# Softmax factors moved from the probabilities to the attention output, with PE spreading them over partitions

## The chip, the cores and the metric

The kernel runs on one core of a Trainium2 chip. The metric is the device time of one execution in microseconds (us). The core has five instruction streams that run beside each other: PE (matrix multiply), DVE (vector), ACT (activation functions), POOL (general vector) and SP (which only issues DMAs here). Each takes its instructions in order; semaphores hold an instruction back until its inputs are there or its buffer is free.

## The reference

Three stages follow each other. With B, H, S, D = 4, 8, 576, 64:

```
scores = q k^T / 8, causal, plus min(-(cum_i - cum_j), 0) with cum = cumsum(max(s, 0))
attn   = exp(scores - max) / (sum + 1e-9)
out    = attn v                                  # [B, H, S, D]
x  = out as [2304, 512]
h  = x @ w_in          [2304, 2048]
x  = (h * cos(h)) @ w_out                        # called FF1 below
xn = x / rms(x) * rms_g
out = (silu(xn @ w_gate) * (xn @ w_val)) @ w_out2  # called FF2 below
```

All inputs are fp32.

## The kernel before

**Tiling.** Attention goes by 16 pairs of heads. A pair has two parts: part a holds the first 256 queries (two tiles of 128 for each of the two heads), part b the other 320 (tiles 2 and 3 of each head, and a tile "p" that stacks the last 64 queries of both heads on the 128 partitions). For each tile PE makes scores (line 430 the product, 435 the bias; 457 and 458 for "p"), DVE copies them out of PSUM and finds the row minimum of the negated scores (442, 461), ACT takes the exponential in place and sums the row (469). The method norm (473) turns the row sums into factors: POOL forms (sum + 1e-9) * 2 pi (477), DVE takes the reciprocal (479), and each tile of exponentials is multiplied in place by its factor, one number to a partition, on DVE (485), ACT (486) or POOL (484). Then PE transposes the scaled tiles (500), ACT or DVE copies the transposes out of PSUM into P, PE multiplies by v (532) so that the output X has the head's 64 channels on partitions (head 0 on 0 to 63, head 1 on 64 to 127) and the queries along the row, and one copy takes X out of PSUM into xu (line 535, recorded under the helper's lines 286 on ACT and 289 on DVE). A DMA stores xu to DRAM.

**FF1** goes by 9 blocks of 256 rows. Its products are lines 634 (x w_in) and 640 (g w_out), each of them three fp32r products (high and low halves). Block 0 needs part a of the first four pairs, so FF1 can begin while attention still runs; PE alternates between the two from then on. During attention the weights of FF1 are also brought from DRAM and split into high and low halves: lines 361 to 371, on ACT or POOL (361, 362), POOL (365), DVE (366, 368) and helpers 286, 289, 293, 297 and 299 (tiles raw, cv, wi, ws). **FF2** goes by 6 blocks of 384 rows, with the same two kinds of product.

**What sets the order.** All work is recorded as operations with a cost in ns for each engine that may do it, a due time and the buffers read and written. A planner (Plan.order) walks through time, gives each operation to the engine that would end it first, and lets each engine take the ready operation with the earliest due time. The result is one fixed instruction order for each engine. Due times of attention advance by P_ATT (ns) per pair, those of FF1 by P_FF1 per unit from T_FF1. Four PSUM banks (4 to 7) serve attention; they are handed out in turn as the program records the operations, so an operation waits until the use of its bank four places earlier is done.

Of the kernel before, what the change touches and what calls it, by code (L numbers as in the profile page):

```python
# [10 lines left out]
F32 = mybir.dt.float32  # L11
F32R = mybir.dt.float32r
I32 = mybir.dt.int32
AF = mybir.ActivationFunctionType
ALU = mybir.AluOpType
# [24 lines left out]
HALF_PI = 1.5707962  # L40
BIG = 1.0e9
SIZES = {"u": 3, "xr": 1, "xa": 3, "xb": 2, "raw": 3, "P32": 4}
P_ATT, P_FF1, P_FF2 = 9000.0, 8093.98, 5800.0
T_FF1 = 45000.0


# [143 lines left out]
def dve1(n):  # L190
    return 1.042 * n + 67


def dve2(n):
    return 0.52 * n + 68


def act_s(n):
    return 0.833 * n + 93
# [6 lines left out]
def pool1(n):  # L206
    return 0.833 * n + 161


def pool2(n):  # L210
    return 2.105 * n + 147
# [3 lines left out]
def attention_moe_moe(ctx, tc, q2, k2, vp, s, w_in, w_out, w_gate, w_val, w_out2, rms_g, out):  # L215
    nc = tc.nc
    pe, act, dve, pool, sp = nc.tensor, nc.scalar, nc.vector, nc.gpsimd, nc.sync
    plan = Plan()

    def spool(stack, name, **kw):  # L220
        return stack.enter_context(tc.tile_pool(name=name, bufs=1, reuse_waits="tile", **kw))
# [3 lines left out]
    psum = spool(ctx, "psum", space=PSUM)  # L225
# [6 lines left out]
    def ring(name, n, shape, dtype, where="main"):  # L232
        n = SIZES.get(name, n)
        def make(slot):
            if where not in pools:
                first, kw = ends[where]
                stacks[first].close()
                pools[where] = spool(ctx, where, **kw)
            return pools[where].tile(shape, dtype, name=f"{name}{slot}", tag=f"{name}{slot}")

        r = Ring(plan, make, n)
        if where in ("main", "x1", "att"):
            for i in range(n):
                r.tile(i)
        return r
# [6 lines left out]
    ident = main.tile([128, 128], F32, name="ident")  # L252
# [27 lines left out]
    def on(e, ns, fn):  # L280
        return [(e, ns, fn)]

    def copy(o, i, n, r, w, scale=1.0, psum=False, engines=("ACT", "DVE", "POOL"), **kw):
        alts = []
        if "ACT" in engines:
            alts.append(("ACT", (act_p if psum else act_s)(n), lambda: act.activation(o(), i(), AF.Copy, scale=scale)))  # L286
        if "DVE" in engines:
            if scale == 1.0:
                alts.append(("DVE", (dve1 if psum else dve2)(n), lambda: dve.tensor_copy(o(), i())))
            else:  # L290
                alts.append(("DVE", dve2(n), lambda: dve.tensor_scalar(out=o(), in0=i(), scalar1=scale, scalar2=None, op0=ALU.mult)))
        if "POOL" in engines and not psum:
            alts.append(("POOL", pool1(n), lambda: pool.tensor_scalar(out=o(), in0=i(), scalar1=scale, scalar2=0.0, op0=ALU.mult, op1=ALU.add)))  # L293
        return plan.op(alts, r, w, **kw)

    def two(o, a, b, n, r, w, op=ALU.subtract, psum=False, **kw):
        alts = on("DVE", dve1(n), lambda: dve.tensor_tensor(out=o(), in0=a(), in1=b(), op=op))  # L297
        if not psum:
            alts += on("POOL", pool2(n), lambda: pool.tensor_tensor(out=o(), in0=a(), in1=b(), op=op))
        return plan.op(alts, r, w, **kw)  # L300
# [42 lines left out]
    xu_r = ring("xu", 3, [128, 320], F32, "att")  # L343
    p32_r = ring("P32", 4, [128, 4, 320], F32, "att")
    mn_r = ring("mn", 2, [128, 10], F32, "att")
    rs_r = ring("rs", 2, [128, 5], F32, "att")
    rn_r = ring("rn", 2, [128, 5], F32, "att")

    DS = {0: (0, 128), 1: (128, 256), 2: (384, 384), 3: (768, 512), "p": (1280, S)}
    x_d = [[{c: dbuf(f"x_d{b}_{p}{c}", [128, n]) for c, n in (("a", 256), ("b", 320))} for p in range(NP)] for b in range(B)]  # L350
# [52 lines left out]
    class Part:  # L403
# [7 lines left out]
            return psb("att", (4, 5, 6, 7))  # L411

        def stats(self):
            self.mn, self.rs, self.rn, self.xu = mn_r.new(), rs_r.new(), rn_r.new(), xu_r.new()

        def score(self, ts):

# [55 lines left out]
        def norm(self, keys):  # L473

            rn, rs, a = self.rn, self.rs, self.col[keys[0]]
            b = a + len(keys)
            plan.op(on("POOL", 204, lambda: pool.tensor_scalar(
                out=rn()[:, a:b], in0=rs()[:, a:b], scalar1=1e-9, scalar2=float(2.0 * np.pi), op0=ALU.add, op1=ALU.mult)), [(rs, self.col[k]) for k in keys], [(rn, a)])
            plan.op(on("DVE", 204, lambda: dve.reciprocal(out=rn()[:, a:b], in_=rn()[:, a:b])), [], [(rn, a)])
            for k in keys:  # L480
                (E, part, o, w), i = self.E[k], self.col[k]
                at, by = (lambda E=E, o=o, w=w: E()[:, o:o + w]), (lambda i=i: rn()[:, i:i + 1])
                plan.op([
                    ("POOL", 2.44 * w + 290, lambda at=at, by=by: pool.tensor_scalar(out=at(), in0=at(), scalar1=by(), scalar2=None, op0=ALU.mult)),
                    ("DVE", 0.62 * w + 110, lambda at=at, by=by: dve.tensor_scalar(out=at(), in0=at(), scalar1=by(), scalar2=None, op0=ALU.mult)),  # L485
                    ("ACT", act_s(w) + 93, lambda at=at, by=by: act.activation(at(), at(), AF.Copy, scale=by())),
                ], [(rn, a)], [(E, part)])

        def tr(self, e, i):
            tr = self.bank("T")  # L490
# [25 lines left out]

        def av(self):

            X, vr, P, n = self.bank("X"), self.run.vr, self.P, self.n

            def go():
                if self.c == "a":
                    ps = [P[e]().rearrange("p c i -> p (c i)") for e in range(2)]
                    jobs = [(0, 128, 0, 256, [p[:, 0:256] for p in ps]), (1, 128, 128, 256, [p[:, 256:384] for p in ps])]
                else:
                    ps = [P[e]() for e in range(2)]
                    jobs = [(c, 128, 0, 320, [p[:, c, :] for p in ps]) for c in range(3)]
                    jobs.append((3, 128, 128, 320, [p[:, 3, 128:320] for p in ps]))
                    jobs.append((4, 128, 256, 320, [p[:, 3, 0:64] for p in ps]))
                for c, kk, lo, hi, p in jobs:  # L530
                    for e in range(2):
                        pe.matmul(X()[64 * e:64 * e + 64, lo:hi], vr()[:kk, e, c, :], p[e], start=(c == 0), stop=(c == jobs[-1][0]))  # L532

            plan.op(on("PE", (640 if self.c == "a" else 2130) + SWITCH_PE, go), [vr, *P.values()], [X])
            copy(lambda: self.xu()[:, :n], lambda: X()[:, :n], n, [X], [self.xu], psum=True)

        def store(self):
            xu, n, xd = self.xu, self.n, x_d[self.run.b][self.run.p][self.c]
# [43 lines left out]
    for b in (s_b, cum):  # L582
# [4 lines left out]
        out=cum()[:, :S], data0=ones.to_broadcast([128, S]), data1=s_b()[:, :S], initial=0.0, op0=ALU.mult, op1=ALU.add)), [(s_b, 0)], [(cum, 0)])  # L587
# [6 lines left out]
    for i, (t, mid) in enumerate(((0, 63), (1, 191), (2, 319), ("p", 543), (3, 447))):  # L594
        o, w = DS[t]
# [9 lines left out]
            out=to(), in0=src(), scalar=halves[:, 1:2], in1=to().bitcast(F32), op0=ALU.mult, op1=ALU.add)), [raw], [(ds, o)], **kw)  # L605
# [75 lines left out]
    for j in range(1, NB1):  # L681
        for f in range(F1):
# [4 lines left out]
            w = w2[j, f] = ws_r.new() if j < RES else wr_r.new(f)  # L687
# [44 lines left out]
    for k in range(8 * NB1):  # L732
        j, m = divmod(k, 8)
# [5 lines left out]
        for i in range(2):  # L739
            plan.now = tick_at(k)  # L740
            w = w1[2 * m + i]
# [8 lines left out]
        for i in range(2):  # L750
            plan.now = tick_at(k) + 1.6 * P_FF1
            f = 2 * m + i
            w = w2[j, f]
# [46 lines left out]
    for n, (d, f, w) in enumerate((d, f, w) for f in range(F2) for d, w in (("g", w_gate), ("v", w_val), ("o", w_out2))):  # L800
# [4 lines left out]
        b = ws_r.new() if n < 4 else slots[n - 4][1].new(slots[n - 4][2])  # L805
# [4 lines left out]
    for n in range(NB2 * F2):  # L810
# [20 lines left out]
        w = w3["o", f]  # L831
# [4 lines left out]
        if f == F2 - 1:  # L836
            plan.now = unit_at(n)
            for t in range(3):
                o = u_r.new()
# [59 lines left out]
```

## Time and profile before

| what | value |
|---|---|
| median of 3 runs | 1107.75 us (1107.7 to 1108.04) |
| the profiled execution's own time | 1110.82 us |
| its span, first to last instruction | 1109.0 us |
| busy: PE, DVE, ACT, POOL | 97%, 49%, 48%, 17% |
| mean granted TensorE clock | 0.992 of full speed |

The span is what the profile shows; the execution's own time has 1.8 us around it. Busy shares are averages over unlike stages: attention, first alone and then with FF1 between its steps (to about 297 us), FF1 alone, and FF2. Matmuls overlap in PE, and their ends are modelled, so that PE shows as busy in stretches where it waits in part; the chain of waits (the instructions that ended last, followed backwards) tells better who set the pace of a stretch.

### The profile page before, as it was taken

The numbers are of one execution on the slowest core, as the hardware profiler recorded it, in microseconds if no ns is written. First come the engines' busy times: TensorE is split into PE (matmuls) and PEld (weight loads), VectorE is DVE, ScalarE is ACT, GpSimd is POOL, SyncE is SP. The second block draws the span as 40 slices with busy tenths as digits, with TensorE's granted clock in tenths as the row PEclk, the third lists the DMA queues.
The fourth block names the chain that finished last, engine by engine and source line by source line (L and its number), as shares of the span: only waits on it lengthen the run. The fifth ranks groups of instructions, "written<-read, shape, count | busy, mean of one in ns | idle before, by whom it ended". The sixth has DMA issues, their size and how long they took to land.

```text
span 1109.0 us, 16861 instructions
## 1 busy us (share of the span) xinstructions
PE 1080.4 (97%) x6474; PEld 938.8 (85%) x6474; DVE 547.1 (49%) x1209; ACT 528.7 (48%) x1098; POOL 187.1 (17%) x256
## 2 busy tenths in 40 slices
PE   8899999999999999999999999999999999999998
PEld 5568667777799999999998788999999999999997
DVE  6887998864474543535438888421211211211211
ACT  4889889988754543444435555321211211211111
POOL 3544556321030000000003444100000000000000
PEclk7999999999999999999999999999999999999999
DMA  5765677743392000000002537110000100100000
GB/s 179 239 205 172 212 252 234 241 142 107 123 390 65 22 27 20 20 29 30 20 20 80 164 120 223 39 57 1 25 34 1 57 1 1 43 1 1 30 1 29
DMA packets 51377, 101.28 MB, mean 91 GB/s; under 512 B 7520, under 2 KB 27488, under 8 KB 51296
## 3 DMA queue, kind: packets, MB, share of 16 engines
q1 hardware_dynamic: 51296, 100.19, 27.4%
q8 instruction: 51, 0.84, 0.3%
q14 instruction: 30, 0.25, 0.1%
HBM read 77.63 MB, written 22.54 MB: 90 GB/s over the span
## 4 chain that ended last, share of the span: by engine, by line
PE 80%; DVE 9%; issue 3%; POOL 3%; ACT 3%; DMA 1%; SPq 0%; DVEq 0%; POOLq 0%; ACTq 0%
PE bank L634 40%; PE bank L640 27%; PE bank L500 4%; PE bank L430 3%; PE bank L532 3%; DVE raw L366 2%; DVE cv L368 2%; POOL raw L365 1%; PE bank L457 1%; ACT cv L362 1%; DVE e L485 1%; PE bank L435 1%; DVE u L297 1%; DVE e L442 1%; PE bank L724 1%
## 5 line engine op out<-in xcount | busy, mean ns | idle before, releaser
L640 PE MATMUL bank<-wr,g 128*128 128x512 f32 x996 | 248.5, 396 | 4.7 <-ACT g L286 3.8
L297 DVE TENSOR_TENSOR u<-bank,u 128x512 f32<-128x512 f32 (+1 forms) x144 | 89.8, 623 | 313.0 <-PE bank L634 235.4
L634 PEld LDWEIGHTS bank<-xa,wi 128*128 128x128 f32 x1728 | 215.2, 188 | 9.1 <-DVE u L297 1.6
L634 PE MATMUL bank<-xa,wi 128*128 128x256 f32 x1728 | 221.3, 283 | 1.6 <-DVE u L297 1.4
L640 PEld LDWEIGHTS bank<-wr,g 128*128 128x128 f32 x996 | 182.6, 188 | 43.5 <-ACT g L286 4.9
L286 ACT ACTIVATE g<-u 128x512 fp32r<-128x512 f32 (+1 forms) x130 | 74.8, 576 | 265.2 <-DVE u L297 265.2
L297 DVE TENSOR_TENSOR g<-u,g 128x512 fp32r<-128x512 f32 (+1 forms) x127 | 82.4, 649 | 69.3 <-ACT g L286 69.2
L634 PE MATMUL bank<-xb,wi 128*128 128x384 f32 x528 | 101.8, 338 | 0.0
L634 PEld LDWEIGHTS bank<-xb,wi 128*128 128x128 f32 x528 | 93.7, 188 | 1.6
L634 PE MATMUL bank<-xb,wr 128*128 128x384 f32 x480 | 92.0, 335 | 0.0
L744 ACT ACTIVATE u<-bank,quarter 128x512 int32<-128x512 f32 x72 | 49.2, 684 | 81.0 <-PE bank L634 79.5
L297 DVE TENSOR_TENSOR u<-u,bank 128x512 f32<-128x512 int32 x72 | 49.3, 685 | 77.7 <-ACT u L744 76.2
L634 PEld LDWEIGHTS bank<-xb,wr 128*128 128x128 f32 x480 | 84.6, 188 | 1.8
L469 ACT ACTIVATE e<-e,mn 128x128 f32<-128x128 f32 (+3 forms) x128 | 70.6, 554 | 13.3 <-DVE mn L442 12.5
L746 ACT ACTIVATE u<-u,half_pi 128x512 f32<-128x512 f32 x72 | 52.1, 724 | 41.1 <-DVE u L297 40.8
L442 DVE CUSTOM_DVE_ANT_0 e<-bank,cm 128x128 f32<-128x128 f32 (+3 forms) x128 | 56.9, 484 | 22.9 <-PE bank L435 22.2
L640 PE MATMUL bank<-wi,g 128*128 128x512 f32 x270 | 66.8, 392 | 0.7 <-ACT g L286 0.7
L293 POOL TENSOR_SCALAR g<-u 128x512 fp32r<-128x512 f32 (+1 forms) x14 | 9.2, 659 | 340.6 <-DVE u L297 340.6
L826 ACT ACTIVATE u<-bank 128x384 f32<-128x384 f32 x72 | 35.2, 489 | 64.6 <-PE bank L634 53.2
L361 POOL TENSOR_SCALAR cv<-raw 128x512 f32<-128x512 f32 x20 | 15.0, 751 | 291.8 <-DVE wi L297 252.7
L640 PE MATMUL bank<-ws,g 128*128 128x512 f32 x246 | 64.0, 401 | 0.0
L365 POOL TENSOR_SCALAR raw<-raw 128x512 f32<-128x512 f32 x68 | 52.3, 770 | 68.0 <-ACT cv L362 65.6
(131 smaller groups left out, 1522.8 us busy)
## 6 DMA issues: line engine op xcount, KB each, us to landing
raw<-in_w_out_dram SPq DMA_DIRECT2D x28, 512.0 KB, 3.9
raw<-in_w_in_dram SPq DMA_DIRECT2D x16, 512.0 KB, 4.7
wo_d<-ws SPq DMA_DIRECT2D x16, 512.0 KB, 4.8
ws<-wo_d SPq DMA_DIRECT2D x16, 512.0 KB, 4.1
wr<-wo_d SPq DMA_DIRECT2D x16, 512.0 KB, 10.2
raw<-in_w_val_dram SPq DMA_DIRECT2D x12, 512.0 KB, 3.7
raw<-in_w_gate_dram SPq DMA_DIRECT2D x12, 512.0 KB, 3.7
qr<-in_q_dram SPq DMA_DIRECT2D x16, 320.0 KB, 4.8
```

Of the source, the lines that this page charges most:

```text
L286: alts.append(("ACT", (act_p if psum else act_s)(n), lambda: act.activation(o(), i(), AF.Copy, scale=scale)))
L297: alts = on("DVE", dve1(n), lambda: dve.tensor_tensor(out=o(), in0=a(), in1=b(), op=op))
L365: plan.op(on("POOL", pool1(512), lambda: pool.tensor_scalar(out=top().bitcast(F32), in0=top().bitcast(F32), scalar1=0.0, scalar2=1.0, op0= ...
L430: pe.matmul(Sp[e]()[:, o:o + w], run.q()[hd, q0:q0 + 128], run.k()[hd, :w], start=(t == ts[0]), stop=False)
L442: plan.op(on("DVE", dve1(w) + 17, lambda o=o, w=w, i=i, e=e: dve.tensor_tensor_reduce(out=Es[e]()[:, o:o + w], in0=Sp[e]()[:, o:o + w], in ...
L469: plan.op(on("ACT", act_s(w) + 187, lambda E=E, o=o, w=w, i=i: act.activation(E()[:, o:o + w], E()[:, o:o + w], AF.Exp, scale=-1.0, bias=s ...
L500: pe.transpose(tr()[:m, 128 * j:128 * j + 128], E[0]()[:, E[2] + c:E[2] + c + m], ident)
L634: pe.matmul(h, w[:, a, 128 * k:128 * k + 128], x[k // 2][:, k % 2, c, :blk], start=(n == 0), stop=(n == 11))
L640: pe.matmul(acc[t], g[a][:, 128 * t:128 * t + 128], w[:, c, :], start=(first and (a, c) == (0, 0)), stop=(last and (a, c) == (1, 0)))
L744: plan.op(on("ACT", act_p(512) + 93, lambda u=u, h=h: act.activation(u().bitcast(I32), h(), AF.Identity, bias=quarter)), [h], [u])
L746: plan.op(on("ACT", act_s(512) + 93, lambda u=u: act.activation(u(), u(), AF.Sin, scale=-TWO_PI, bias=half_pi)), [], [u], table="sin")
L826: plan.op(on("ACT", act_p(BLK2), lambda us=us, h=hs[0]: act.activation(us(), h()[:, :BLK2], AF.Silu)), [hs[0]], [u], table="silu")
```

## The change

The exponentials are no longer multiplied. norm still lets POOL form the scaled sums; DVE now takes the reciprocal with an output that repeats each factor 64 times along the row (tile rb, 256 or 128 numbers to a partition), and for "p" also one plain reciprocal (128x1). In the method av a new PE step (factors) transposes rb through the identity into a bank R, which puts the factor of every query along the row, on all 64 partitions of its head; for "p", whose two heads share the partitions, two small products with the identity do the same. R is copied to xu, and the copy of X out of PSUM becomes a multiplication of X by xu on DVE. The order is planned anew, with the new costs and P_ATT of 9500 in place of 9000.

```diff
--- before.py
+++ after.py
@@ -40,7 +40,7 @@
 HALF_PI = 1.5707962
 BIG = 1.0e9
 SIZES = {"u": 3, "xr": 1, "xa": 3, "xb": 2, "raw": 3, "P32": 4}
-P_ATT, P_FF1, P_FF2 = 9000.0, 8093.98, 5800.0
+P_ATT, P_FF1, P_FF2 = 9500.0, 8093.98, 5800.0
 T_FF1 = 45000.0
 
 
@@ -345,6 +345,7 @@
     mn_r = ring("mn", 2, [128, 10], F32, "att")
     rs_r = ring("rs", 2, [128, 5], F32, "att")
     rn_r = ring("rn", 2, [128, 5], F32, "att")
+    rb_r = ring("rb", 2, [128, 2, 2, 64], F32, "att")
 
     DS = {0: (0, 128), 1: (128, 256), 2: (384, 384), 3: (768, 512), "p": (1280, S)}
     x_d = [[{c: dbuf(f"x_d{b}_{p}{c}", [128, n]) for c, n in (("a", 256), ("b", 320))} for p in range(NP)] for b in range(B)]
@@ -411,7 +412,7 @@
             return psb("att", (4, 5, 6, 7))
 
         def stats(self):
-            self.mn, self.rs, self.rn, self.xu = mn_r.new(), rs_r.new(), rn_r.new(), xu_r.new()
+            self.mn, self.rs, self.rn, self.rb, self.xu = mn_r.new(), rs_r.new(), rn_r.new(), rb_r.new(), xu_r.new()
 
         def score(self, ts):
 
@@ -476,15 +477,16 @@
             b = a + len(keys)
             plan.op(on("POOL", 204, lambda: pool.tensor_scalar(
                 out=rn()[:, a:b], in0=rs()[:, a:b], scalar1=1e-9, scalar2=float(2.0 * np.pi), op0=ALU.add, op1=ALU.mult)), [(rs, self.col[k]) for k in keys], [(rn, a)])
-            plan.op(on("DVE", 204, lambda: dve.reciprocal(out=rn()[:, a:b], in_=rn()[:, a:b])), [], [(rn, a)])
-            for k in keys:
-                (E, part, o, w), i = self.E[k], self.col[k]
-                at, by = (lambda E=E, o=o, w=w: E()[:, o:o + w]), (lambda i=i: rn()[:, i:i + 1])
-                plan.op([
-                    ("POOL", 2.44 * w + 290, lambda at=at, by=by: pool.tensor_scalar(out=at(), in0=at(), scalar1=by(), scalar2=None, op0=ALU.mult)),
-                    ("DVE", 0.62 * w + 110, lambda at=at, by=by: dve.tensor_scalar(out=at(), in0=at(), scalar1=by(), scalar2=None, op0=ALU.mult)),
-                    ("ACT", act_s(w) + 93, lambda at=at, by=by: act.activation(at(), at(), AF.Copy, scale=by())),
-                ], [(rn, a)], [(E, part)])
+            rb, p = self.rb, "p" in keys
+            if self.c == "a":
+                o, i = (lambda: rb()), (lambda: rn()[:, :4].rearrange("p (e t) -> p t e", e=2))
+            else:
+                t = 0 if p else 1
+                o, i = (lambda: rb()[:, t:t + 1]), (lambda: rn()[:, a:a + 2].unsqueeze(1))
+            m = 1 if self.c == "b" else 2
+            plan.op(on("DVE", 128 * m + 80, lambda: dve.reciprocal(out=o(), in_=i().unsqueeze(3).to_broadcast([128, m, 2, 64]))), [(rn, a)], [(rb, a)])
+            if p:
+                plan.op(on("DVE", 150, lambda: dve.reciprocal(out=rn()[:, 2:3], in_=rn()[:, 2:3])), [], [(rn, a)])
 
         def tr(self, e, i):
             tr = self.bank("T")
@@ -516,7 +518,20 @@
 
         def av(self):
 
-            X, vr, P, n = self.bank("X"), self.run.vr, self.P, self.n
+            R, X, vr, P, n = self.bank("R"), self.bank("X"), self.run.vr, self.P, self.n
+            rn, rb = self.rn, self.rb
+
+            def factors():
+
+                if self.c == "b":
+                    i = self.col["p"]
+                    for e in range(2):
+                        pe.matmul(R()[64 * e:64 * e + 64, 256:320], rn()[:, i:i + 1].to_broadcast([128, 64]), ident[:, 64 * e:64 * e + 64], start=True, stop=True)
+                for t in range(2):
+                    pe.transpose(R()[:, 128 * t:128 * t + 128], rb()[:, t].rearrange("p e m -> p (e m)"), ident)
+
+            plan.op(on("PE", 218 + (300 if self.c == "b" else 0), factors), [rn, rb], [R], rows=0.5)
+            copy(lambda: self.xu()[:, :n], lambda: R()[:, :n], n, [R], [self.xu], psum=True)
 
             def go():
                 if self.c == "a":
@@ -532,7 +547,7 @@
                         pe.matmul(X()[64 * e:64 * e + 64, lo:hi], vr()[:kk, e, c, :], p[e], start=(c == 0), stop=(c == jobs[-1][0]))
 
             plan.op(on("PE", (640 if self.c == "a" else 2130) + SWITCH_PE, go), [vr, *P.values()], [X])
-            copy(lambda: self.xu()[:, :n], lambda: X()[:, :n], n, [X], [self.xu], psum=True)
+            two(lambda: self.xu()[:, :n], lambda: X()[:, :n], lambda: self.xu()[:, :n], n, [X], [self.xu], op=ALU.mult, psum=True)
 
         def store(self):
             xu, n, xd = self.xu, self.n, x_d[self.run.b][self.run.p][self.c]
```

First PE, where the third pair's score tile "p" is made (457, 458, in two halves) between the second pair's last transposes (500, with the operand ident) and its product with v (532, first of ten rows), before:

```order
L500 MATMUL bank_154<-ident,e_173 128x128 x4
L457 MATMUL bank_155<-kr_159,qr_157 128x288
L458 MATMUL bank_155<-ds_165,pk_161 128x288
L500 MATMUL bank_156<-ident,e_172 128x128 x4
L457 MATMUL bank_153<-kr_159,qr_157 128x288
L458 MATMUL bank_153<-ds_165,pk_161 128x288
L532 MATMUL bank_154<-P_181,vr_164 64x320
```

and the same place in the changed order, where the lines are 458, 459, 502 and 547:

```order
L458 MATMUL bank_154<-kr_159,qr_157 128x288
L459 MATMUL bank_154<-ds_165,pk_161 128x288
L529 MATMUL bank_153<-ident,rn_188 64x64 x2
L531 MATMUL bank_153<-ident,rb_190 128x128 x2
L502 MATMUL bank_155<-ident,e_172 128x128 x4
L458 MATMUL bank_156<-kr_159,qr_157 128x288
L459 MATMUL bank_156<-ds_165,pk_161 128x288
L547 MATMUL bank_154<-P_181,vr_164 64x320
```

The new step (529 and 531, into bank_153) belongs to the second pair; it stands between the two halves of "p", ahead of a transpose and of the product with v, so that all of these are queued behind it on PE.

Then DVE, in the middle of the fourth pair: before, reciprocals (479) and multiplications of exponentials (485) among score copies (442, 461) and weight steps (366, 368):

```order
L479 RECIPROCAL rn_187<-rn_187 128x4
L442 ISA e_170,mn_184<-bank_155,cm_166 128x384
L442 ISA mn_184 128x1
L485 TENSOR_SCALAR e_169<-e_169,rn_187 128x128
L485 TENSOR_SCALAR e_169<-e_169,rn_187 128x256
L461 ISA ep_174,mn_184<-bank_153,cp_167 128x288
L461 ISA mn_184 128x1
L461 ISA ep_174,mn_184<-bank_155,cp_167,mn_184 128x288
L461 ISA mn_184 128x1
L289 COPY pk_162<-pick 128x128
L366 SCALAR_TENSOR_TENSOR raw_131<-raw_131 128x512
L479 RECIPROCAL rn_188<-rn_188 128x3
```

and now, where 487 and 489 are the reciprocals, 443 and 462 the score copies, 367 and 369 the weight steps, and xu the multiplication at the end of a part:

```order
L487 RECIPROCAL rb_189<-rn_187 128x256
L369 SCALAR_TENSOR_TENSOR cv_133<-cv_133,raw_130 128x512
L367 SCALAR_TENSOR_TENSOR raw_131<-raw_131 128x512
L462 ISA ep_174,mn_184<-bank_156,cp_167,mn_184 128x288
L462 ISA mn_184 128x1
L297 TENSOR_TENSOR ws_128<-cv_133,ws_128 128x512
L369 SCALAR_TENSOR_TENSOR cv_132<-cv_132,raw_131 128x512
L487 RECIPROCAL rb_190<-rn_188 128x128
L489 RECIPROCAL rn_188<-rn_188 128x1
L297 TENSOR_TENSOR xu_178<-bank_154,xu_178 128x320
L297 TENSOR_TENSOR wi_113<-cv_132,wi_113 128x512
L443 ISA e_173,mn_184<-bank_156,cm_166 128x512
```

The multiplications of e are gone from DVE; the reciprocals stand in the same places and write 256 or 128 numbers to a partition in place of 4 or 3, and a multiplication of xu that reads PSUM has come in.

## Rows read from the trace of the kernel before

**Rows 1.** The page: the whole chain by engine.
```profile
PE 80%; DVE 9%; issue 3%; POOL 3%; ACT 3%; DMA 1%; SPq 0%; DVEq 0%; POOLq 0%; ACTq 0%
```
**Rows 2.** Busy us by stage, first column from and to; instructions in brackets.
```profile
core 0: us, PE busy (x) PEld busy (x) DVE busy (x) ACT busy (x) POOL busy (x), PEclk, DMA share, GB/s
13.90:83.90 70.00, 63.28 (x393) 41.84 (x393) 53.81 (x157) 57.74 (x161) 30.03 (x46) 0.88 0.60 193
83.90:194.00 110.10, 106.19 (x734) 79.77 (x733) 96.41 (x247) 97.84 (x223) 59.17 (x79) 1.00 0.64 217
194.00:297.00 103.00, 103.00 (x746) 77.99 (x747) 63.36 (x204) 91.89 (x217) 20.58 (x38) 1.00 0.47 150
297.00:500.00 203.00, 203.00 (x1308) 184.19 (x1305) 98.39 (x181) 93.18 (x154) 9.34 (x10) 1.00 0.24 86
```
**Rows 3.** The chain's shares in 13.9 to 83.9, 83.9 to 194, 194 to 297.
```profile
by line: PE bank L500 19.7%; PE bank L430 16.5%; PE bank L532 11.9%; DMA qr<-in_q_dram 8.3%; issue 7.7%; PE bank L435 4.3%; PE bank L457 3.6%; DVE e L442 3.3%; DVE raw L366 3.2%; DVE e L485 2.5%; POOL raw L365 2.2%; ACT e L469 2.1%; POOL rn
...
by line: PE bank L500 9.7%; PE bank L634 9.1%; issue 8.2%; PE bank L640 7.9%; PE bank L430 7.1%; DVE e L485 6.3%; DVE raw L366 5.1%; DMA raw<-in_w_out_dram 4.7%; PE bank L532 4.2%; DVE cv L368 3.6%; DVE e L442 3.1%; POOL raw L365 2.5%; ACT 
...
by line: PE bank L500 21.6%; PE bank L532 19.4%; PE bank L634 17.2%; PE bank L640 17.1%; PE bank L430 14.4%; PE bank L457 4.7%; PE bank L435 3.4%; PE bank L458 1.3%; PE bank L724 1.0%
```
**Rows 4.** Pieces of the chain: start, us, what.
```profile
32.64 0.62 POOL rn L477
...
56.06 0.61 ACT e L486
...
170.63 0.59 POOL rn L477
...
199.98 0.80 PE bank L532 x8
...
202.36 0.87 PE bank L500 x8
...
213.30 2.21 PE bank L532 x20
```
**Rows 5.** Line 485 on DVE by stage, with the sum.
```profile
13.90:83.90 70.00, 9.14 (x18) 0.88 0.60 193
83.90:194.00 110.10, 17.94 (x31) 1.00 0.64 217
...
sum 283.10, DVE 37.77; mean DVE 12.59
```
**Rows 6.** Line 486 on ACT, sum of the same stages.
```profile
sum 283.10, ACT 37.47; mean ACT 12.49
```
**Rows 7.** Line 479 on DVE, the first two stages.
```profile
13.90:83.90 70.00, 2.38 (x14) 0.88 0.60 193
83.90:194.00 110.10, 2.90 (x17) 1.00 0.64 217
```
**Rows 8.** Groups by form, 0 to 420 us: shapes, count | busy us, mean ns.
```profile
L442 DVE CUSTOM_DVE_ANT_0 e<-bank,cm 128x384 f32<-128x384 f32 x32 | 16.8, 550 | 9.5 <-PE bank L435 9.4
L442 DVE CUSTOM_DVE_ANT_0 e<-bank,cm 128x256 f32<-128x256 f32 x32 | 12.3, 418 | 0.0
L286 ACT ACTIVATE xu<-bank 128x320 f32<-128x320 f32 x16 | 6.7, 418 | 0.1
L479 DVE RECIPROCAL rn<-rn 128x4 f32<-128x4 f32 x16 | 2.8, 174 | 2.2 <-POOL rn L477 2.0
L479 DVE RECIPROCAL rn<-rn 128x3 f32<-128x3 f32 x16 | 2.8, 172 | 8.7 <-POOL rn L477 8.5
L479 DVE RECIPROCAL rn<-rn 128x2 f32<-128x2 f32 x16 | 2.7, 167 | 7.8 <-POOL rn L477 7.2
L289 DVE COPY xu<-bank 128x256 f32<-128x256 f32 x2 | 0.8, 416 | 2.1 <-PE bank L532 2.1
```

## The prediction, made before the changed kernel was run

> **What bounds the kernel now.** I read the chain of waits first, whole and then by stage, because busy shares mix stages. Over the span 80% of the chain lies on PE [rows 1], so that most of the kernel pays for PE work at its full price. The stages differ. From 194 to 297 us every entry of the chain is a PE line [rows 3], though ACT is busy for 91.9 of the 103 us [rows 2]: here an extra us of PE work is an extra us of time. From 297 on there is only FF1 and then FF2, whose work the change leaves as it is. From 13.9 to 194 us the five PE lines shown add up to 56% and 38% of the two stretches, 39.2 + 41.8 = 81 of 180.1 us, or 45% [rows 3]; the rest is on DVE and POOL, on ACT and on transfers, and DVE and ACT are busy for 150.2 and 155.6 us of these 180.1 [rows 2]. So before 194 us DVE counts, after it PE. The lines to be removed show it: the multiplications on DVE (485) are 2.5% and 6.3% of the chain, 1.75 + 6.94 = 8.7 us [rows 3], out of 27.1 us that they are busy there [rows 5]. A us of DVE work thus cost 0.32 us of time. The same work on ACT (486) has one piece of 0.61 us in the chain [rows 4]; its 37.5 us [rows 6] are nearly all hidden.
>
> **PE, added.** A part gets two transposes of 128x128: eight take 0.87 us [rows 4], two 0.218. Part b also gets two products of 64 columns on the two halves of the array. The nearest row is the product with v of part b, 20 instructions in 2.21 us [rows 4], which is ten such pairs with 320 x 3 + 192 + 64 = 1216 columns, 1.82 ns each; 64 columns are 0.116 us. So a and b get 0.218 and 0.334 us. In the order before, ten a and nine b products with v have begun by 194 us, six and seven are left (the first of these pieces are in [rows 4]). After 194: 6 x 0.218 + 7 x 0.334 = 3.65 us, all on the chain. Before: 10 x 0.218 + 9 x 0.334 = 5.19 us at PE's 45% of the chain, 2.3 us. The bounds of this second term are 0 (PE waits there anyway) and 5.2.
>
> **DVE, removed and added, for all 16 pairs.** Gone: line 485, 37.8 us, and line 479, 2.8 + 2.8 + 2.7 = 8.3 us [rows 5, 8]. The multiplication of X reads 320 or 256 numbers from PSUM like the score copies, 418 ns at 256 and 550 at 384 [rows 8], so 1.03 ns a number and 484 ns at 320: 16 x (0.484 + 0.418) = 14.4 us. Of the copies of R the new order gives five to DVE, 4 x 0.484 + 0.416 = 2.4 us, where two of xu cost 0.8. Together 16.0 us more.
>
> The reciprocals are the open price: 16 of 256 numbers, 32 of 128 and 16 of one, where 16 each of 4, 3 and 2 stood. They took 174, 172 and 167 ns [rows 8], a slope of (174 - 167) / 2 = 3.5 ns a number. No reciprocal of a long row is in the trace, so there are bounds. Low: 1.03 ns a number, as every copy; then 434 and 302 ns, and with 0.16 for the single ones 6.9 + 9.7 + 2.6 = 19.2 us. High: the copies' fixed part is 418 - 256 x 1.03 = 154 ns, and all that the three short reciprocals take above it is per number, (167 - 154) / 2, (172 - 154) / 3, (174 - 154) / 4, about 6 ns; then 1690 and 922 ns, 59.1 us in all. I take the slope of the reciprocal's own rows, the nearest: 174 + 252 x 3.5 = 1056 and 608 ns, 16.9 + 19.5 + 2.6 = 39.0 us, which is 30.7 more than line 479.
>
> The three rows leave the price open between 1 and 6 ns a number [rows 8]. The Trainium skill (VectorE: DVE Perf Modes, section Walkthrough: the 8-slice pipeline in each mode) says that Reciprocal runs as a hardware divide with a repeat count of 8. Eight passes at the copies' 1.03 ns would be 8.2 ns a number, an estimate of 77 us for all reciprocals and about 1143 us for the kernel; the slope in this trace is less than half of it, and no run here shows a long one.
>
> By 194 us 31 of the 48 reciprocals are done [rows 7], 0.646 of the pairs. So before 194 DVE gets (30.7 + 16.0) x 0.646 = 30.2 us and loses 27.1, +3.1 us; at 0.32 that is +1.0 us. After 194 DVE is idle for 40 of 103 us [rows 2], which hides it.
>
> **ACT and POOL.** ACT loses line 486 and keeps as many copies out of PSUM as before, of R in place of X (418 ns at 320 [rows 8]): -0.6 us, what line 486 has in the chain. In the new order ACT and DVE also take over weight steps from POOL, which eats a part of what ACT gets; that is why I count no more.
>
> **The path from the exponentials to the transposes** no longer goes through POOL and the reciprocal. POOL's step (477) has five pieces in the chain before 194, from 0.62 us at 32.64 to 0.59 at 170.63 [rows 4], 3.2 us by all five. The factor is still needed, but only for R, so I take three quarters: -2.4 us. Bounds: 0 and -3.2.
>
> **The new wait.** The transposes of rb stand in PE's fixed order, with the second half of "p", transposes and the product with v queued behind them, and DVE and ACT wait for those. The planner books 128 m + 80 ns, 336 or 208, for a reciprocal; at 1056 and 608 the factor is 0.72 or 0.40 us later than booked, over 32 parts at most 17.9 us of PE waiting, at least nothing, since other work stands ahead of them. The nearest row has PE waiting for DVE at a few places only (no DVE line but 442, 366 and 485 is large in [rows 3]); I take 1.0 us.
>
> **Pace.** P_ATT shifts FF1 against attention, but in both orders 28 first products of FF1 stand ahead of the last product with v, and 24 before against 25 now of the second: nothing by the end of attention.
>
> **Sum.** 3.65 + 2.3 + 1.0 - 0.6 - 2.4 + 1.0 = +5.0 us. The profiled execution took 1110.8 us, its span 1109.0; it lies 3.1 us (0.28%) above the median of the runs, 1107.75, and would become 1115.8. The same difference on the median gives 1112.8 us.
>
> **Rivals.** First, faster: the reciprocal runs at the copies' 1.03 ns a number. DVE then gets (10.9 + 16.0) x 0.646 = 17.4 us before 194 and loses 27.1, -9.7 us. At 0.32 that is -3.1, at full price -9.7; DVE's 83% busy before 194 [rows 2] speaks for more than 0.32, the middle, 0.66, is -6.4. With no late factors: 3.65 + 2.3 - 6.4 - 0.6 - 2.4 = -3.4, 1104.3 us. It decides below 2 ns a number (a 256 in some 0.6 us), where DVE's relief pays for PE. Against it stands the slope of [rows 8]. Second, much slower: the reciprocal costs 6 ns a number. DVE gets (50.8 + 16.0) x 0.646 = 43.2 us, +16.1, and is busy for 166 of 180 us. It is then the bound, each us at full price, and the factors come 1.35 and 0.71 us later than booked, of whose 33 us I take 4: 5.0 - 1.0 - 1.0 + 16.1 + 4 = +23, 1131 us. With DVE's work at 0.32 and no late factors it would be 1116. For it: three short rows all lie above the copies' line. Against: they rise by 3.5, not 6. A third way, that before 194 us nothing moves because weights and transfers hold DVE (a transfer has 8.3% and 4.7% of the two stretches [rows 3]), leaves +3.65, 1111.4 us; it is part of the forecast's own spread.
>
> **How the numbers follow.** Two runs of this kernel are told apart from about 0.2%, 2.2 us. Forecast 0.40 (slower 0.32, same 0.08), fast reciprocal 0.30 (faster 0.21, same 0.09), slow reciprocal 0.30 (slower 0.29, same 0.01): faster 0.21, same 0.18, slower 0.61. The forecast's own range is 1107 to 1118. The range of 8 in 10 runs from 1103, which leaves out the fast rival at DVE's full price, to 1136, the second rival with 9 instead of 4 of the 33 us of late factors.
>
> **What would show it.** Lines 485 and 486 gone; reciprocals of 256 near 1.06 us and of 128 near 0.61 (0.43 and 0.30 for the first rival, 1.7 and 0.92 for the second); multiplications of xu near 0.48 and 0.42; eight transposes still 0.87 us, and the last product with v some 5 us later than before, with the chain all on PE in the last third of attention. DVE's busy time up to then would be 3 us above 150 (140 and 166 for the rivals). I am wrong if DVE's reciprocals appear in the chain for more than some 5 us, or if PE's waiting before 194 shrinks by more than the 6 us that it is given to do.

## The result and the profile after

The changed kernel takes 1118.56 us (median of 4 runs, 1118.44 to 1118.72) against 1107.89 us (4 runs, 1107.7 to 1110.34) for the kernel before, run beside it: ratio 1.0088, 95% interval 1.0075 to 1.0102. It is 10.7 us slower. The forecast was 1112.8: right in sign and within its range, 5.8 us too low.

The span of the profiled execution grew by 7.7 us, to 1116.7. The other 3 us are the kernel before's: its profiled execution lay 3.1 us above its median, and in 13.9 to 83.9 us its granted clock was 0.88 [rows 2], where after has 1.00.

Line numbers after: 431, 436, 458, 459 make scores, 443 and 462 copy them out, 487 and 489 are the reciprocals, 529 and 531 the new PE step, 502 the transposes, 547 the product with v, 649 and 655 FF1 (and FF2), 297 on xu the new multiplication. First the whole chain by engine, as [rows 1]:

```profile
PE 81%; DVE 10%; issue 3%; ACT 2%; POOL 2%; DMA 1%; POOLq 0%; DVEq 0%; ACTq 0%
```

Hardly anything moved there. Then busy time by stage, as [rows 2]:

```profile
core 0: us, PE busy (x) PEld busy (x) DVE busy (x) ACT busy (x) POOL busy (x), PEclk, DMA share, GB/s
13.90:83.90 70.00, 62.64 (x450) 41.85 (x451) 61.28 (x153) 51.72 (x148) 30.32 (x45) 1.00 0.66 215
83.90:194.00 110.10, 106.17 (x752) 78.74 (x752) 100.28 (x234) 97.25 (x222) 41.72 (x61) 1.00 0.60 204
194.00:297.00 103.00, 102.86 (x733) 77.17 (x729) 68.85 (x186) 76.83 (x184) 11.26 (x26) 1.00 0.47 149
```

DVE is busy for 161.6 of the 180.1 us before 194, against 150.2 before the change, although the multiplications of exponentials are gone from it. The chain's shares of the first two stretches, as [rows 3], suggest that this matters:

```profile
by line: issue 16.8%; DVE e L443 9.7%; DVE rb L487 9.2%; PE bank L502 7.6%; PE bank L547 7.5%; DVE cv L369 7.0%; DMA raw<-in_w_out_dram 5.7%; PE bank L431 4.2%; PE bank L649 4.1%; DVE raw L367 3.7%; DVE P L289 2.7%; ACT P L286 2.2%; DVE ep 
...
by line: issue 11.2%; PE bank L547 7.8%; DVE cv L369 6.6%; DVE raw L367 5.6%; DVE rb L487 5.6%; DVE e L443 5.4%; PE bank L649 5.3%; PE bank L502 5.3%; DVE ws L297 4.3%; PE bank L655 3.8%; PE bank L431 3.3%; ACT cv L363 2.7%; DVE u L297 2.5%
```

Transposes and the product with v were 31.6% of the first stretch (500 and 532) and are 15.1%; DVE's lines have taken much of their place, and the reciprocal (487) alone has 9.2% of 70.0 and 5.6% of 110.1 us, 6.4 + 6.2 = 12.6 us. "issue" grew as well, from 7.7% and 8.2% [rows 3] to 16.8% and 11.2%, 14.4 to 24.1 us. Much of it is the reciprocal again. Three pieces of the chain in a row, and the instruction that DVE runs meanwhile:

```profile
14.10 0.06 DVE rb L487
14.16 1.53 issue
15.69 0.41 DVE ep L462
...
14.03 1.74 DVE L487 RECIPROCAL rb<-rn 128x256 f32<-128x256 f32 x1
```

The chain leaves the reciprocal for a semaphore that the next instruction waited for, and calls the time until DVE is free "issue". Summed over the pieces of "issue" that lead to a DVE instruction, DVE is running line 487 in 5.0 us of the first stretch and 5.4 us of the second. So the reciprocals hold some 23 us of the chain.

The groups by form, as [rows 8] (count | busy us, mean ns | idle before), say why:

```profile
L487 DVE RECIPROCAL rb<-rn 128x128 f32<-128x128 f32 x32 | 30.3, 945 | 9.6 <-POOL rn L478 9.1
L487 DVE RECIPROCAL rb<-rn 128x256 f32<-128x256 f32 x16 | 28.0, 1747 | 3.8 <-POOL rn L478 3.6
...
L531 PE MATMUL bank<-ident,rb 128*128 128x128 f32 x64 | 13.3, 289 | 0.0
L297 DVE TENSOR_TENSOR xu<-bank,xu 128x320 f32<-128x320 f32 x16 | 7.7, 480 | 2.1 <-PE bank L547 1.8 <-ACT e L470 0.2
...
L297 DVE TENSOR_TENSOR xu<-bank,xu 128x256 f32<-128x256 f32 x16 | 6.7, 417 | 7.1 <-ACT e L470 5.4 <-PE bank L547 0.9 <-issue 0.5
...
L529 PE MATMUL bank<-ident,rn 128*64 128x64 f32 x64 | 5.4, 245 | 0.2
...
L489 DVE RECIPROCAL rn<-rn 128x1 f32<-128x1 f32 x16 | 1.9, 118 | 0.0
```

The reciprocals take 28.0 + 30.3 + 1.9 = 60.2 us, where 39.0 were forecast and 8.3 stood before.

To see where time goes I read three marks from each trace: when the 20th and the 32nd (last) product with v start on PE, and when eight of the transposes that make FF2's input (724, now 739) first stand in a row. From the last mark on, after stays 7.7 us behind before up to the seventh such set (616.1 and 623.9 us), so that all of the loss lies ahead of it. In brackets: first and second products of FF1 done; one of each costs PE 1.6 and 1.5 us in before's trace. The rows from the third on are the experiments below.

| kernel | 20th | 32nd | FF2's first eight |
|---|---|---|---|
| before | 194.5 (16, 12) | 295.1 (28, 24) | 337.0 |
| after | 192.8 (15, 12) | 304.0 (28, 25) | 344.7 |
| short reciprocal | 184.5 (15, 12) | 294.2 (28, 25) | 335.0 |
| no PE step, long reciprocal | 193.5 (15, 12) | 303.1 (28, 25) | 343.8 |
| no PE step, short reciprocal | 180.8 (15, 12) | 287.8 (28, 25) | 328.5 |
| new way in 20 parts, old in 12 | 184.6 (15, 12) | 288.6 (28, 25) | 329.3 |
| no spreading on DVE | 185.1 (15, 12) | 298.1 (28, 25) | 338.8 |

Up to the 20th product after is level with before: 1.7 us earlier, with one first product (1.6 us) less done, and some 3 us worse if the 3.1 us that before's profiled execution has above its median lie there, where its clock was low (that they do is not shown). Then twelve parts take 111.2 us against 100.6, with one more product of each kind done (3.1 us): 7.5 us more.

### The profile page after: what moved, and what is told of

It reads as the page before. It is cut to its first block, busy times and chain, and to the rows that moved or that the text cites. A ratio compares the mean times of both kernels' runs of the same rounds, so it can differ in the third digit from the quotient of the medians.

```text
span 1116.7 us, 17070 instructions
## 1 busy us (share of the span) xinstructions
PE 1088.8 (98%) x6602; PEld 944.5 (85%) x6602; DVE 565.4 (51%) x1178; ACT 512.4 (46%) x1062; POOL 160.2 (14%) x227
## 4 chain that ended last, share of the span: by engine, by line
PE 81%; DVE 10%; issue 3%; ACT 2%; POOL 2%; DMA 1%; POOLq 0%; DVEq 0%; ACTq 0%
PE bank L649 42%; PE bank L655 28%; PE bank L547 3%; PE bank L502 3%; DVE cv L369 2%; PE bank L431 2%; DVE raw L367 2%; DVE e L443 1%; DVE rb L487 1%; DVE u L297 1%; PE bank L739 1%; PE bank L458 1%; POOL raw L366 1%; DVE ws L297 0%; PE bank L436 0%
## 5 line engine op out<-in xcount | busy, mean ns | idle before, releaser
L487 DVE RECIPROCAL rb<-rn 128x128 f32<-128x128 f32 (+1 forms) x48 | 58.1, 1213 | 13.3 <-POOL rn L478 12.7
L286 ACT ACTIVATE P<-bank 128x384 f32<-128x384 f32 (+3 forms) x134 | 52.4, 422 | 23.8 <-PE bank L502 23.0
```

The lines of the kernel that those rows point to most:

```text
L487: plan.op(on("DVE", 128 * m + 80, lambda: dve.reciprocal(out=o(), in_=i().unsqueeze(3).to_broadcast([128, m, 2, 64]))), [(rn, a)], [(rb, a)])
```

## The experiments

Theory 1 was that the long reciprocals are the loss; the rivals were the new PE step with what it holds up, and the other pace.

**Short reciprocal, change's order kept.** The reciprocal is taken in place on 4 or 2 numbers, and a copy repeats it.

```diff
-dve.reciprocal(out=o(), in_=i().unsqueeze(3).to_broadcast([128, m, 2, 64]))
+dve.reciprocal(out=rn()[:, c0:c1], in_=rn()[:, c0:c1])
+dve.tensor_copy(o(), i().unsqueeze(3).to_broadcast([128, m, 2, 64]))
```

> The changed kernel, its order kept, but each long reciprocal (256 or 128 numbers to a partition) becomes a short one in place (4 or 2 numbers) and a DVE copy that repeats the result 64 times. Theory 1, the reciprocals' length on DVE: DVE loses some 38 us (58 us of long reciprocals against 8 us of short ones and 12 us of copies), two thirds of it before 200 us, where a DVE us costs 0.3 to 0.66 us: 1102 to 1110 us. Theory 2, PE's added steps are the whole cost and DVE's load is hidden: within 2 us of the changed kernel's 1118.6.

1107.86 us (10 runs, 1106.75 to 1108.6), ratio to before 0.9993 [0.9983, 1.0003]: all 10.7 us are given back by this edit alone. Its groups:

```profile
L491 DVE COPY rb<-rn 128x128 f32<-128x128 f32 x32 | 11.5, 358 | 1.3
L491 DVE COPY rb<-rn 128x256 f32<-128x256 f32 x16 | 6.0, 374 | 0.6
L490 DVE RECIPROCAL rn<-rn 128x2 f32<-128x2 f32 x32 | 5.2, 162 | 11.7 <-POOL rn L478 11.1
L490 DVE RECIPROCAL rn<-rn 128x4 f32<-128x4 f32 x16 | 2.8, 173 | 3.8 <-POOL rn L478 3.6
...
L495 DVE RECIPROCAL rn<-rn 128x1 f32<-128x1 f32 x16 | 2.5, 154 | 0.0
```

28.0 us in place of 60.2: 10.7 us of time for 32.2 us of DVE, 0.33 for each, taken over the whole of attention. The chain of 83.9 to 194 us (first fence; this run's chain can be followed back only to 60.4 us) and the busy times of the first two stretches (second) turned over to PE:

```profile
by line: PE bank L508 18.5%; PE bank L661 16.0%; PE bank L553 15.5%; PE bank L655 14.8%; PE bank L431 13.4%; PE bank L458 5.4%; PE bank L436 3.2%; PE bank L537 3.1%; issue 1.7%; PE bank L535 1.4%; PE bank L459 1.4%; POOL wi L299 1.2%; DVE e
```

```profile
13.90:83.90 70.00, 67.54 (x479) 45.36 (x478) 54.83 (x177) 54.48 (x153) 30.95 (x46) 0.97 0.66 216
83.90:194.00 110.10, 109.47 (x792) 81.81 (x791) 97.58 (x263) 100.24 (x233) 44.79 (x64) 1.00 0.68 226
```

PE is busy for 177.0 of the 180.1 us, against 168.8 after the change.

**The PE step left out**, xu filled from a constant tile, so that the factors are not applied; with the long reciprocals, and with the short ones.

```diff
-plan.op(on("PE", 218 + (300 if self.c == "b" else 0), factors), [rn, rb], [R], rows=0.5)
-copy(lambda: self.xu()[:, :n], lambda: R()[:, :n], n, [R], [self.xu], psum=True)
+plan.op(on("PE", 218 + (300 if self.c == "b" else 0), lambda: None), [rn, rb], [R], rows=0.5)
+copy(lambda: self.xu()[:, :n], lambda: cm()[:, :n], n, [R], [self.xu], psum=True)
```

> The changed kernel with the PE step of the factors left out (no transposes of rb, no small products; xu is filled by a copy from a constant tile instead of R, so the factors are not applied); the long reciprocals stay. Theory 1: only PE's own 8 to 9 us go, at full price after 194 us and half before, and the waits for late factors with them: 1110 to 1113 us. Theory 2: all 10.7 us go, 1107 to 1109.

> Both edits: short reciprocals with a copy, and no PE step of the factors (which are not applied). Theory 1: the two gains add up nearly, 1096 to 1104 us. Theory 2: the same as without the PE step alone, 1107 to 1109.

| us | short reciprocal | long reciprocal |
|---|---|---|
| without the PE step | 1102.91, ratio 0.9958 [0.9941, 0.9974] | 1118.38, ratio 1.009 [1.0073, 1.0107] |
| with it | 1107.86 | 1118.56 |

The run with long reciprocals missed its expectation: beside them the PE step costs nothing that can be measured (0.2 us, where the interval of that run is 1.9 us to either side); beside short ones it costs 5.0. The two costs do not add. Busy time of the first two stretches, without the step and with long reciprocals:

```profile
13.90:83.90 70.00, 59.66 (x400) 39.35 (x400) 60.71 (x152) 51.01 (x147) 30.68 (x45) 0.98 0.64 207
83.90:194.00 110.10, 102.52 (x715) 77.17 (x715) 99.27 (x233) 96.55 (x219) 42.22 (x61) 1.00 0.61 208
```

PE does 6.6 us less there, DVE nearly as much as with the step, and the 20th product with v stands at 193.5 us, no earlier: PE only waits longer. In this run nothing on PE waits for the factors either, so that late factors are no measurable part of the loss; what is left is DVE's time itself.

**The change at the old pace**, P_ATT 9000.

> The changed kernel with the pace of attention P_ATT back at 9000, which makes the planner order anew. Theories 1 and 2: within 3 us of 1118.6, since neither the reciprocals nor PE's steps change. Theory 3, the pace is what costs: 1108 to 1113 us.

1127.5 us (1126.23 to 1128.11), ratio 1.0175 [1.0159, 1.019]: worse by 9, a miss. At the last product with v FF1 has (26, 23) done, not (28, 25). In 330 to 350 us PE, after the change never idle there, is busy for 16.51 us, at a clock of 0.91, right behind 30 us in which transfers fill 0.88 of the DMA engines:

```profile
300.00:330.00 30.00, 30.00 (x208) 26.73 (x207) 14.38 (x22) 13.10 (x21) 2.18 (x4) 1.00 0.88 341
330.00:350.00 20.00, 16.51 (x103) 14.58 (x103) 10.71 (x17) 9.82 (x17) 3.57 (x4) 0.91 0.45 167
```

What PE waits for there was not followed further. So going back to the old pace gives none of the loss back; with this change it costs more.

**The reciprocal by itself**, on rows of 1 to 512 numbers, and copies of the same rows; nothing else runs (line 56 plain, 59 one number read again and again, 62 the copy).

> Only a row of DVE reciprocals of 1 to 512 numbers to a partition, then of 64, 128 and 256 read with stride 0, then plain copies of 1 to 512; the rest of the kernel is left out. Theory 1a, a price per number that holds at every length: 6.3 ns a number on some 140 ns, so 256 numbers 1.75 us with either input, 512 some 3.35 us, and four numbers 25 ns more than one. Theory 1b, the stride-0 input is what is slow: plain reciprocals of 256 near 0.4 us, only the stride-0 ones 1.75 us.

```profile
L56 DVE RECIPROCAL dst<-one 128x512 f32<-128x512 f32 x4 | 13.4, 3353 | 0.1
L56 DVE RECIPROCAL dst<-one 128x256 f32<-128x256 f32 x4 | 7.0, 1753 | 0.1
L59 DVE RECIPROCAL dst<-one 128x256 f32<-128x256 f32 x4 | 7.0, 1753 | 0.1
...
L62 DVE COPY dst<-one 128x512 f32<-128x512 f32 x4 | 1.7, 427 | 0.1
...
L62 DVE COPY dst<-one 128x256 f32<-128x256 f32 x4 | 1.2, 294 | 0.1
L56 DVE RECIPROCAL dst<-one 128x16 f32<-128x16 f32 x4 | 1.0, 253 | 0.1
...
L56 DVE RECIPROCAL dst<-one 128x4 f32<-128x4 f32 x4 | 0.7, 178 | 0.1
...
L56 DVE RECIPROCAL dst<-one 128x2 f32<-128x2 f32 x4 | 0.7, 166 | 0.1
L56 DVE RECIPROCAL dst<-one 128x1 f32<-128x1 f32 x4 | 0.7, 164 | 0.1
```

(3353 - 253) / 496 = 6.25 ns a number, on 153 ns; every length but 1 lies within 1 ns of that line. A repeated input changes nothing. Rows of 2 and 4 differ by 12 ns here, by 7 in the kernel before (167 and 174 [rows 8]): some ns in the means of short rows had halved the slope.

**The kernel before with the long reciprocals added**, order kept: behind each of the 48 short reciprocals one whose result is not used.

```diff
 dve.reciprocal(out=rn()[:, a:b], in_=rn()[:, a:b])
+dve.reciprocal(out=scratch[:, :m], in_=above_one[:, 0:1].to_broadcast([128, m]))   # m = 256 or 128
```

> The kernel before, its order kept, with one more reciprocal behind each of its 48: 16 of 256 and 32 of 128 numbers into an unused tile, 58 us of DVE work that nobody waits for. Theory 1 (a DVE us costs what the changed kernel paid for it, 10.7 us for 29.3 us of DVE work, 0.37): +21 us, 1129, and more where DVE saturates before 194 us, up to 1145. Theory 2 (DVE's work is hidden): within 4 us of 1108.

1135.55 us (1133.52 to 1137.39), ratio 1.0242 [1.0218, 1.0265]. The added instructions take 57.2 us and cost 27.5, 0.48 for each. A part of that may be PE's clock: in 83.9 to 194 and 194 to 297 us it was granted 0.96 and 0.98, where before has 1.00. The added groups:

```profile
L485 DVE RECIPROCAL scratch<-ones 128x128 f32<-128x128 f32 x32 | 29.7, 927 | 0.0
L485 DVE RECIPROCAL scratch<-ones 128x256 f32<-128x256 f32 x16 | 27.5, 1722 | 0.0
```

**The kernel before at the new pace**, P_ATT 9500.

> The kernel before with P_ATT 9500 alone, ordered anew. Theory 1: the pace shifts work but adds none, 1104 to 1113 us. Theory 3, the pace is what costs the changed kernel its last third: 1112 to 1118.

1110.37 us (10 runs, 1108.66 to 1116.46), ratio 1.002 [1.0002, 1.0038]: some 2 us, hardly to be told from nothing.

**Short reciprocal, the repeating copy free to go to any engine**, planned anew; 38 of the 48 copies go to ACT.

> The changed kernel with short reciprocals on DVE and the repeated copy of the factors as an operation of its own that the planner may give to ACT, DVE or POOL (38 of 48 go to ACT), ordered anew, P_ATT 9500. Theory 1: DVE another 8 us lighter than with the copy on DVE, ACT 11 us busier: 1102 to 1109 us. Theory 2: 1116 to 1120, as PE's steps are unchanged.

1110.24 us (10 runs, 1109.54 to 1112.57), ratio 1.0016 [1.0004, 1.0029]. A miss by 1 us, and no better than leaving the copies on DVE; the order is another one too.

**The new way where DVE and ACT are short, the old way where PE is.** The marks say that with the short reciprocal the 20th product with v comes 10 us earlier than before (with one FF1 product less done), and that the last twelve parts lose it again. So the first ten pairs (20 parts) use the new way with the short reciprocal, the last six the old one; planned anew.

```diff
+late = self.bp >= 10
...
-plan.op(on("PE", 218 + (300 if self.c == "b" else 0), factors), [rn, rb], [R], rows=0.5)
+if not late:
+    plan.op(on("PE", 218 + (300 if self.c == "b" else 0), factors), [rn, rb], [R], rows=0.5)
```

> The short reciprocal with the new way of applying the factors in the first 20 of the 32 parts, and the old way (exponentials multiplied) in the last 12; the planner makes a new order. Theory 1 (up to the 20th product with v DVE and ACT are short, after it PE is; the new way relieves the first and burdens the second): with the short reciprocal everywhere the 20th product stood at 184.5 us against 194.5 before with one FF1 pair of products less done, 8 us of gain, and the last 12 parts then took 109.7 us against 100.6. With the old way there the gain is kept: 1107.9 - 8 = 1100, 1098 to 1103. Rival (the gain by the 20th product is only work put off, which any order gives back later): 1106 to 1110, as with the short reciprocal everywhere.

1102.22 us (1100.97 to 1102.85), ratio 0.9935 [0.9921, 0.9948]: faster than both kernels, 5.9 us below before, and as expected. Up to the 20th product it is the run with the short reciprocal (184.6 and 184.5 us); the last twelve parts take 104.0 us in place of 109.7. The chain of 194 to 297 us is PE alone, without the new step:

```profile
by line: PE bank L678 20.5%; PE bank L519 19.9%; PE bank L672 19.8%; PE bank L567 16.7%; PE bank L431 13.4%; PE bank L458 4.9%; PE bank L436 3.1%; PE bank L459 1.3%; PE bank L762 0.8%
```

**The same at the old pace**, P_ATT 9000.

> The same, planned at the old pace of 9000. Theory 1: within 3 us of the run at 9500, so 1097 to 1106. Theory that a mismatch of the pace with the work left after attention costs as it did at 9000 with the change as given (+9 us): 1105 to 1115.

1109.93 us (11 runs, 1108.75 to 1111.88), ratio 1.0012 [1.0003, 1.0022]. Theory 1 missed here, the pace theory hit: the last product with v stands at 287.8 us, as early as at 9500, but with (26, 24) of FF1 done in place of (28, 25), and FF2's first eight come at 338.5 in place of 329.3 us.

**No spreading on DVE at all**: short reciprocal, change's order, PE reads each factor's column 64 times.

```diff
-pe.transpose(R()[:, 128 * t:128 * t + 128], rb()[:, t].rearrange("p e m -> p (e m)"), ident)
+for e in range(2):
+    pe.matmul(R()[64 * e:64 * e + 64, 128 * t:128 * t + 128], col(t, e), ident, start=True, stop=True)
```

> Short reciprocal, and no DVE copy that repeats it: PE multiplies the identity's 128 columns by the factor's column read 64 times, one product for each head and row tile, in place of a transpose of the copied factors; the order is the change's. DVE loses 48 copies of 0.23 to 0.29 us (12 us of busy time, at 0.37 us of time each -4.4 us); PE gives up 64 transposes and does 64 pairs of 128-column products instead, for which the pair of 64 columns (0.26 us) gives 0.26 to 0.52 us a pair against 0.22: +0.1 to +0.6 us in each of 32 parts, all of it in 12 parts and 0.45 of it in 20. Theory 1: 1107.9 - 4.4 + 2 to 13 = 1105 to 1116, most likely 1109. Rival (DVE's time alone decides, PE's is hidden as it was beside the long reciprocals): 1103 to 1104.

1112.84 us (1111.66 to 1114.25), ratio 1.0035 [1.0023, 1.0047], 5.0 us over the short reciprocal with copies. 17.5 us of copies (12 were expected) are gone from DVE, 13.0 of them up to the 20th product with v, which comes no earlier (185.1 against 184.5 us); the last twelve parts take 113.0 in place of 109.7. The same edit makes PE's step longer: in the last twelve parts it takes 7.4 us in place of 4.2, start to start, 0.27 more for a part, and at that price 5.4 more up to the 20th product (an estimate). So the lighter DVE may have given back up to 4.8 us there, 0.37 for each, which PE's added work spent again; this run does not tell the two apart. With short reciprocals PE has no time left to wait in:

```profile
83.90:194.00 110.10, 109.97 (x850) 81.93 (x850) 91.58 (x237) 98.84 (x231) 44.11 (x64) 1.00 0.67 227
```

## Why the prediction came out as it did

**The reciprocals: the step that failed.** The sum took 3.5 ns a number, the slope of rows of 2, 3 and 4 numbers; it is 6.25. 1747 and 945 ns were measured, 1056 and 608 forecast. The upper bound, 1690 and 922 ns, was nearly exact: it had taken all that the short rows had above the copies' fixed part as per number. Three means within 7 ns of each other were read as a line to 256. The Trainium skill (VectorE: DVE Perf Modes, section Walkthrough: the 8-slice pipeline in each mode) gives the reciprocal's divide a repeat count of 8. Read in the prediction as eight passes at the price of the PSUM copies, 8.2 ns a number, it comes out too high: 6.25 ns are six times the 1.03 ns of those copies.

**The price of a DVE us: too low, and charged in too few places.** The sum took 0.32 from line 485's part in the chain, for DVE work before 194 us, and nothing after. The short reciprocal's 0.33 is another quantity, over all 32.2 us. Up to the 20th product with v, reciprocals and copies went from 37.6 to 19.5 us of DVE, and the product came 8.3 us earlier: 0.46 for each. The other 14.1 us lie after it and gave 1.5 us. For the same edit the sum would have had 18.1 x 0.32 = 5.8 us. The reading was low in part for the reason shown above: in the trace before, 2.0 us of "issue" are time in which DVE runs line 485, so that it held 10.7 of 27.1 us, or 0.39. The second rival, right on the reciprocal (1690 and 922 ns), was too dear at 1131 with each us at full price; its other figure, 1116 at 0.32 with no late factors, was nearer than the forecast. With the measured reciprocals the forecast's own sum would have had 38.6 us (lines 487 and 489 in the first two stretches) in place of 0.646 x 39.0 = 25.2, 13.4 x 0.32 = 4.3 more: +9.3, 1117.1. DVE's busy time to 194 us, 161.6, lies between the 153 of the forecast and the 166 of that rival.

**PE's step: the size nearly held, its place in the sum did not.** After the 20th product with v the trace has it, start to start, at 2.6 us for 24 transposes and 1.6 us for six pairs, 4.2 us against the 3.65 of the sum (which had a part more); a pair of 64 columns takes 0.26 us, not 0.116. With short reciprocals the step costs 5.0 us, against 3.65 + 2.3 in the sum; with the long ones it costs nothing, since PE waits for DVE anyway. The forecast added it to the reciprocals' cost. That its sum came out low only by 5.8 us, within its range, is thus partly luck: the reciprocals were too cheap in it, and PE's step before 194 us too dear. The marks divide the loss otherwise than the sum: up to the 20th product nothing in the trace, or some 3 us with what before's clock may have cost, against 1.3 in the sum; after it 7.5 against 3.65.

**The last third: the cost was there, and larger.** The chain there was to be all PE, and the last product with v 5 us late. It came 8.9 us late, and the chain of 194 to 297 us has 2.7% of "issue" and 2.0% of line 443 on DVE:

```profile
by line: PE bank L502 18.3%; PE bank L547 16.5%; PE bank L649 15.6%; PE bank L655 15.4%; PE bank L431 14.7%; PE bank L458 3.7%; PE bank L436 3.5%; PE bank L531 3.2%; issue 2.7%; DVE e L443 2.0%; PE bank L529 1.3%; PE bank L739 1.1%; PE bank
```

Where 3.65 us were forecast, 7.5 were found. With the old way in the last twelve parts they are 5.7 us shorter, of which the new instructions have 4.2; the rest, 1.5 us, is in the other PE steps of the new order. Another 1.5 us (111.2 against 109.7) goes with the long reciprocals, which DVE's 40 idle us were to hide.

**Hits.** The multiplications of xu took 480 and 417 ns (484 and 418 forecast). Lines 485 and 486 are gone. The mark "wrong if reciprocals have more than some 5 us of the chain" was the one that fell, with 12.6 under their own line alone: by its own test the prediction was wrong, though the time came within its range; PE's waiting before 194 us did not shrink (10.6 to 11.3 us).

**The other rivals.** The first (a fast reciprocal, 1104.3) can be held against the short reciprocal: 28.0 us of DVE instead of its 19.2, and 1107.86. Its gain before 194 us is there (the 20th product 10.0 us earlier than before, with one first product of FF1, 1.6 us, less done; 3.1 us of it may be before's clock), and the last third spends it again. The third, that nothing moves before 194 us, describes the marks, but by two effects that cancel: the short reciprocal moves the 20th product by 8 us.

**Open.** The term for the path without POOL (-2.4) was not measured apart, and neither was the bank that R takes out of the turn of four: every run that applies the new way to all parts has it. Why the kernel before did about as well at either pace, and the changed one did not, was seen only in FF1's progress, not taken apart. A threshold other than ten pairs was not tried. A new order by itself moves the time: at 9000 in place of 9500 the kernel with the old way in the last six pairs is 7.7 us slower, and the changed one 8.9. How much of the 5.9 us of that run would stay with another order is open; the marks show that the last twelve parts got shorter by 5.7 us.

## What to carry to other kernels

Price an instruction at the length in which it will run: a slope from rows of two to four numbers hangs on a few ns and says little about 256. Take costly functions on the short row, and repeat the result afterwards. An engine's load has a price only in the stage that it bounds, so two loads on engines that wait for each other don't add; try each edit in the stages apart, and fit the pace again. In a chain of waits, look at what the engine runs during "issue" before you read a line's share.

## What the runs showed of the hardware that was not expected

DVE's reciprocal costs 153 ns and 6.25 ns a number, 3353 ns for 512, where a copy takes 427. Two products of 64 columns on the two halves of the array take 0.26 us, more than two transposes of 128x128 (0.22 us start to start). DVE's copy of 256 factors took 374 ns in the kernel and 294 alone; why was not looked into. A us of DVE work taken away by the short reciprocal gave 0.46 us up to the 20th product with v and some 0.11 after it, where PE fills nearly all of the chain.
